# Local attention in units of 32 queries with 128 keys, all 8 heads in one piece

## The chip, the core and the metric

The kernel runs on one core of one Trainium2 chip. The metric is the device time of one launch in microseconds (us), median of three runs. The kernel works on five engines with a queue each: PE (TensorE, matmuls; its weight loads are shown as PEld), DVE (VectorE), ACT (ScalarE), POOL (GpSimd) and SP (SyncE), which here issues nearly all DMA transfers.

## The reference

```python
B, H, Sl, D, Sg = 4, 8, 512, 64, 32; window = 32; scale = 1 / np.sqrt(D)
# global queries see all keys, local queries see the global keys and |i - j| <= 32
s_g = scale * q_g @ concat(k_g, k_l).T;  out_g = softmax(s_g) @ concat(v_g, v_l)
s_ll = np.where(mask, scale * q_l @ k_l.T, -1e9)
s_l = concat(scale * q_l @ k_g.T, s_ll)
out_l = softmax(s_l) @ concat(v_g, v_l)
x = concat(out_g, out_l) as [2176 tokens, 512]
# first feed-forward: d_model 512, d_ff 2048
h = x @ w_in;  y = (h * tanh(softplus(h))) @ w_out
# then 8 experts of 272 tokens each: a greedy assignment by the logits y @ w_gate,
# and relu(y @ w1[e]) @ w2[e] for the tokens of each expert
```

All is float32. The change touches `out_l` alone.

## The kernel before

Phase 1 (the function `phase1`, here 0 to some 310 us) does the attention and the first half of the first feed-forward (8 of 16 rows of 128 hidden units) for six of its blocks; phase 2 (to some 500 us) does the rest of that feed-forward; then come the routing and the experts. Everything behind phase 1 is untouched by the change and runs off what phase 1 leaves.

The 2048 local queries are 16 tiles of 128 (t = 0 to 15). A tile is worked in two **pieces** of 4 heads (`piece(t, g)`). A piece has stages, each ended by a `yield`: (q) scores psS = Q K^T of 128 queries with 224 keys (its own 128, 32 global, 32 on either side), one matmul a head, two heads at a time in the two halves of the array's rows (L357); (t) DVE adds the mask and takes the row's maximum (L367); (e, f) ACT takes exp and the row's sum (L371); (n) DVE divides the probabilities by the sum (L375 to L378); (a, A, b, B) PE transposes them, in 128 and 96 keys, and ACT copies each set of four to SBUF (L382 to L392); (v) the product with v as weights, two matmuls a head, gives the output transposed in psX (L401, L402); (y) ACT and DVE split it into a high and a low float32r part, xh and xl (`x_parts`, L343, L345). Eight pieces for the global queries (`piece_g`) stand between them.

The weights of the feed-forward come as 16 loads of 512 KB in phase 1 (`load_wide`): a DMA into one of three buffers `wide` (L215), three DVE instructions that unpack (L220 to L222), and a split on ACT and POOL (L195, L198). A **chunk** is a quarter of a block's feed-forward: matmuls into psH (L509), a chain on ACT and DVE (L517 to L535) and matmuls into psY (L543). It is given to PE in four **units**; its weights must have been loaded. A **gate** multiplies a finished block's tile by w_gate (L268 to L280).

The order of work is a loop in `phase1` (L649) over the pieces, with a table `SEQ` (`SEQ1` for the first NS = 7 rounds) of what to emit in a round: "4z" is stage z of the piece begun four rounds ago, "u" a unit, "g" a gate's step, "w" idle matmuls that keep PE awake. RATE (L662) says how many units a round may emit, LDR and LDR1 (L659) how many loads. In the first NS rounds PE, ACT and DVE work in the order of emission, after them PE alone does; the other two are ordered by a scheduler. SP keeps its own order, and a DMA that waits holds those behind it.

Of the kernel before, what the change touches and what calls it, by code (L numbers as in the profile page):

```python
# [24 lines left out]
WIN = 32  # L25
TOP = -(1 << 30)
# [15 lines left out]
CH0 = 6  # L42
RATE = 0.667
LDR1 = 1.1
LDR = 1.5
LAG = 1
XTRA = 6
WK = ["001", "301", "113", "211"]
CHAIN = 5
SEQ = "4z u 2A 0n u 2B 3x g U"  # L50
SEQ1 = "0q w 1f 2a 2A w 3v 0t 3y 3x 1n w 2b 0e 2B"
STAGES = "qtefnaAbBvyxz"
NS = 7
# [18 lines left out]
def constants():  # L72
    c = {}
    c["ident"] = np.eye(128)
    c["triu"] = np.triu(np.ones((128, 128)), 1)
    c["off"] = np.tile(np.arange(KT) - (KT - 1) // 2, (128, E))
    c["ecol"] = np.tile(np.arange(E) * 256, (128, 1))
    c["eadj"] = np.tile(REST - 256 - np.arange(E) * (256 - CAP + 256), (128, 1))
    c["iob"] = np.tile(np.r_[0:256, REST:REST + 128], (128, 1))
    c["ioa"] = np.tile(np.arange(NT) * 128, (128, 1))  # L80
    row = token_rows()
    c["rhi"] = row // 128
    c["rlo"] = row % 128
    c["frev"] = (N * E - (row[:, :, None] * E + np.arange(E))).reshape(128, -1)
    i = np.arange(128)[:, None]
    mask = []
    for first, last in ((True, False), (False, False), (False, True)):
        j = np.arange(128)[None]
        r = np.arange(32)[None]
        ok = np.concatenate([abs(i - j) <= WIN, np.ones((128, SG), bool),  # L90
                             (i <= r) & (not first), (r <= i - 96) & (not last)], 1)
        mask.append(np.where(ok, 0.0, NEG))
    c["mask"] = np.concatenate(mask, 1)
# [12 lines left out]
def lay_out(q_l, k_l, v_l, q_g, k_g, v_g):  # L106
    qk = np.zeros((B, 4, 128, 4, 352), np.float32)
    v = np.zeros((B, 4, 128, 2, DM), np.float32)
    qg = np.zeros((B, 2, 128, 2, SG), np.float32)
    kt = np.zeros((B, 2, 128, 2, SL + SG), np.float32)  # L110
    vt = np.zeros((B, 2, 128, 4, 256), np.float32)

    def pairs(a):
        return a.reshape(B, 4, 2, a.shape[2], D).transpose(0, 2, 4, 1, 3).reshape(B, 128, 4, a.shape[2])

    def rows(a):
        return a.transpose(0, 2, 1, 3).reshape(B, a.shape[2], DM)

    ql, kl, kg = pairs(q_l), pairs(k_l), pairs(k_g)
    vl, vg = rows(v_l), rows(v_g)  # L120
    for c in range(4):
        s = c * 128
        qk[:, c, :, :, 0:128] = ql[..., s:s + 128]
        qk[:, c, :, :, 128:256] = kl[..., s:s + 128]
        qk[:, c, :, :, 256:288] = kg
        v[:, c, :, 0] = vl[:, s:s + 128]
        v[:, c, 0:32, 1] = vg
        if c > 0:
            qk[:, c, :, :, 288:320] = kl[..., s - 32:s]
            v[:, c, 32:64, 1] = vl[:, s - 32:s]  # L130
        if c < 3:
            qk[:, c, :, :, 320:352] = kl[..., s + 128:s + 160]
            v[:, c, 64:96, 1] = vl[:, s + 128:s + 160]
    qa = pairs(q_g)
    for g in range(2):
        qg[:, g] = qa[:, :, 2 * g:2 * g + 2]
        kt[:, g, :, :, :SL] = kl[:, :, 2 * g:2 * g + 2]
        kt[:, g, :, :, SL:] = kg[:, :, 2 * g:2 * g + 2]
        vt[:, g] = vl[:, :, g * 256:(g + 1) * 256].reshape(B, 4, 128, 256).transpose(0, 2, 1, 3)
    return {"qk": qk, "v": v, "qg": qg, "kt": kt, "vt": vt}  # L140


class Build:
# [203 lines left out]
    def piece(s, t, g):  # L347
# [14 lines left out]
        mx = s.sp.tile([128, 4], F32, name="mx")
        sm = s.sp.tile([128, 4], F32, name="sm")
        for hp in range(2):
            for j in range(2):
                h = 2 * hp + j
                s.link(nc.vector.tensor_tensor_reduce(out=P[:, h], in0=psS[j][:, hp], in1=mask, scale=-SCALE, scalar=3e38,  # L367
                                                      op0=OP.add, op1=OP.min, accum_out=mx[:, h:h + 1]))
        yield "t"
        for h in range(4):  # L370
            s.link(nc.scalar.activation(P[:, h], P[:, h], AF.Exp, bias=mx[:, h:h + 1], scale=-1.0,  # L371
                                        accum_out=sm[:, h:h + 1]))
            if h > 0:
                yield " eef"[h]
        s.link(nc.vector.tensor_scalar(sm, sm, 1e-9, None, op0=OP.add))  # L375
        s.link(nc.vector.reciprocal(sm, sm))
        for h in range(4):
            s.link(nc.vector.tensor_scalar(P[:, h], P[:, h], sm[:, h:h + 1], None, op0=OP.mult))  # L378
        yield "n"
        psA = s.psT.tile([128, 4, 128], F32, name="psA", tag="t")  # L380
        for h in range(4):
            s.link(nc.tensor.transpose(psA[:, h], P[:, h, 0:128], s.ident))  # L382
        yield "a"
        PA = s.ap.tile([128, 4, 128], F32, name="PA")
        s.link(nc.scalar.activation(PA, psA, AF.Copy))
        yield "A"
        psB = s.psT.tile([96, 4, 128], F32, name="psB", tag="t")
        for h in range(4):
            s.link(nc.tensor.transpose(psB[:, h], P[:, h, 128:224], s.ident))
        yield "b"  # L390
        PB = s.ap.tile([96, 4, 128], F32, name="PB")
        s.link(nc.scalar.activation(PB, psB, AF.Copy))  # L392
        yield "B"
        if g == 0:
            s.px = s.psT.tile([128, 4, 128], F32, name="psX", tag="x")
        px, v = s.px, s.V[t]
        for h in range(4):
            hp, j = 2 * g + h // 2, h % 2
            d0 = (2 * hp + j) * 64
            o = px[j * 64:(j + 1) * 64, hp]  # L400
            s.link(nc.tensor.matmul(o, v[:, 0, d0:d0 + 64], PA[:, h], start=True, stop=False))  # L401
            s.link(nc.tensor.matmul(o, v[:96, 1, d0:d0 + 64], PB[:, h], start=False, stop=True))  # L402
        if g == 0:
            return
# [26 lines left out]
    def load_gv(s, i):  # L431
# [7 lines left out]
        nc.sync.dma_start(vg, vd[b, 0, 0:32, 1, g * 256:(g + 1) * 256])  # L439
        s.gv = v, vg  # L440

    def piece_g(s, i):
# [16 lines left out]
        P = s.ap.tile([128, 544], F32, name="Pg", tag="P", bufs=3)  # L459
# [11 lines left out]
        PA = s.ap.tile([128, 4, 128], F32, name="PgA", tag="PA")  # L471
# [5 lines left out]
        PB = s.ap.tile([32, 128], F32, name="PgB", tag="PB")  # L477
# [108 lines left out]
    def phase1(s, p1):  # L586
# [3 lines left out]
        for t in range(16):  # L590
            pieces += [("l", t, 0), ("l", t, 1)] + [("g", i) for i, a in enumerate(GLOBALS) if a == t]
        chunks = [(bi, f) for bi in range(6) for f in range(0, FP, 2)]
        with ExitStack() as at:
# [18 lines left out]
            s.mask = s.gp.tile([128, 3, 224], F32, name="mask")  # L612
# [33 lines left out]
            n = sent = 0  # L646
            acc = 0.0
            old = []
            while pieces or old:  # L649
# [5 lines left out]
                new = None  # L655
                if pieces:
                    p = pieces.pop(0)
                    new = s.piece(*p[1:]) if p[0] == "l" else s.piece_g(p[1])
                while loads and sent <= (n * LDR1 if n < NS else NS * LDR1 + (n - NS) * LDR):  # L659
                    s.side.append(loads.pop(0))  # L660
                    sent += 1
                acc = min(acc + RATE * 4, 6) if n >= CH0 else 0  # L662
# [3 lines left out]
                w = iter(WK[n] if n < len(WK) else ())  # L666
                for op in (SEQ1 if n < NS else SEQ).split():
                    if op == "w":
                        idle(int(next(w, 0)))
# [6 lines left out]
                    elif op == "g":  # L676
                        if s.gates:
                            g = s.gates[0]
                            s.gate((s.at.get(g, 0),))
                            if s.at[g] == 1:  # L680
                                s.gate((1,))
                    elif int(op[0]) < len(old) and old[int(op[0])]:
# [3 lines left out]
                s.turn_all(s.side)  # L686
                while old and (len(old) > 4 or (old[-1] is None)):
                    old.pop()
                if n == 1:
                    s.load_v(1)  # L690
                    nc.sync.dma_start(s.wg[:, :4 * E].rearrange("p (k e) -> p k e", e=E), s.ins["wg"].rearrange("(k p) e -> p k e", p=128))
                if n == 4:
# [543 lines left out]
```

## Time and profile before

| | us |
|---|---|
| runs: median (lowest to highest of 3) | 862.93 (860.92 to 863.78) |
| the profiled execution: its time / its span | 863.93 / 862.1 |
| PE busy over the span | 801.1 (93%) |
| DVE, ACT, POOL busy | 580.5 (67%), 455.9 (53%), 170.5 (20%) |
| HBM read / written | 91.00 MB / 19.66 MB |

Busy time of matmuls is the union of their modelled spans, so a PE that reads 99% may still have matmuls further apart than they need be; what a group of matmuls costs is read from the start of the first to the start of what follows. An f32 matmul stands in the trace as two instructions (a transpose as one).

### The profile page before, as it was taken

What the parts mean: (1) busy time and instruction counts of PE and PEld (TensorE: products, weight loads), DVE (VectorE), ACT (ScalarE), POOL (GpSimd) and SP (SyncE); (2) the same over time, 40 slices, a digit from 0 to 9 for tenths busy, and PEclk for the clock granted to TensorE, in tenths of its full rate; (3) what the DMA queues carried; (4) which work ended last, traced back from release to release, by engine and by line L of the source; (5) the groups of instructions that cost most, each with busy time, mean ns of one, the idle gap of its engine ahead of it and who ended that gap; (6) DMA issues with size and microseconds to landing.
All of it is one profiled execution on the core that took longest, in us unless ns stands there. A gap on an engine that the chain in (4) does not pass through costs nothing. (4 is left out here: it accounts for less than half of the span.)

```text
span 862.1 us, 16222 instructions
## 1 busy us (share of the span) xinstructions
PE 801.1 (93%) x6276; PEld 688.6 (80%) x6276; DVE 580.5 (67%) x1467; ACT 455.9 (53%) x987; POOL 170.5 (20%) x138
## 2 busy tenths in 40 slices
PE   8787999999999999979999997899879899999995
PEld 4565777777777888868999876677679899999994
DVE  6999866656666458797877868886646565564420
ACT  5676666666676656556555653222246454454320
POOL 1222100000000012243100146644330221222001
PEclk9899999999999999999999999999999999999998
DMA  9768635344441002343131114423557646665101
GB/s 316 252 212 283 201 135 170 100 145 125 161 137 52 25 25 74 99 133 100 50 97 52 51 49 140 62 29 46 159 152 242 218 139 229 208 210 194 50 8 55
DMA packets 44720, 111.74 MB, mean 130 GB/s; under 512 B 5728, under 2 KB 14304, under 8 KB 44640
## 3 DMA queue, kind: packets, MB, share of 16 engines
q1 hardware_dynamic: 37696, 91.01, 32.5%
q0 software_dynamic: 6944, 19.67, 9.0%
q8 instruction: 50, 0.82, 0.4%
q14 instruction: 30, 0.25, 0.1%
HBM read 91.00 MB, written 19.66 MB: 128 GB/s over the span
## 5 line engine op out<-in xcount | busy, mean ns | idle before, releaser
L517 ACT ACTIVATE me<-psH 128x512 f32<-128x512 f32 (+1 forms) x72 | 41.0, 570 | 60.0 <-PE psH L509 59.9
L371 ACT ACTIVATE P<-P,mx 128x224 f32<-128x224 f32 x128 | 60.1, 470 | 19.6 <-DVE mx L367 19.1
L519 DVE TENSOR_SCALAR mu<-me 128x512 f32<-128x512 f32 (+1 forms) x72 | 34.9, 484 | 36.7 <-ACT me L517 35.6
L522 ACT ACTIVATE me<-mu,two 128x512 f32<-128x512 f32 (+1 forms) x72 | 49.9, 693 | 15.5 <-DVE mu L520 15.0
L525 DVE TENSOR_TENSOR mu<-mu,psH 128x512 f32<-128x512 f32 (+1 forms) x72 | 46.9, 652 | 10.9 <-ACT me L522 10.8
L367 DVE CUSTOM_DVE_ANT_0 P<-psS,mask 128x224 f32<-128x224 f32 x128 | 43.1, 385 | 8.8 <-PE psS L357 8.6
L520 DVE SCALAR_TENSOR_TENSOR mu<-me,mu 128x512 f32<-128x512 f32 (+1 forms) x72 | 47.6, 661 | 1.9
L1190 DVE SCALAR_TENSOR_TENSOR hl<-ps2H,hh 128x272 fp32r<-128x272 f32 x64 | 27.0, 437 | 27.9 <-ACT hh L1189 27.9
L1189 ACT ACTIVATE hh<-ps2H 128x272 fp32r<-128x272 f32 x64 | 24.8, 395 | 38.9 <-PE ps2H L1187 38.8
L198 POOL TENSOR_TENSOR wo10l<-wz,wo10h 128x512 fp32r<-128x512 f32 x2 | 2.6, 1323 | 214.0 <-ACT wo10h L195 214.0
L523 ACT ACTIVATE me<-me 128x512 f32<-128x512 f32 (+1 forms) x72 | 43.6, 606 | 1.5
L357 PE MATMUL psS<-qk 64*128 64x224 f32 x256 | 38.9, 384 | 3.6 <-DVE L L583 2.3
L378 DVE TENSOR_SCALAR P<-P,sm 128x224 f32<-128x224 f32 x128 | 36.9, 351 | 1.0
L1204 ACT ACTIVATE oT<-ps2O 128x256 f32<-128x256 f32 x32 | 12.1, 378 | 41.9 <-PE ps2O L1202 41.9
L357 PEld LDWEIGHTS psS<-qk 64*128 64x128 f32 x256 | 24.8, 190 | 11.8 <-issue 4.5
L1168 POOL DMA_INDIRECT out<-ro,idx x17 | 21.4, 1259 | 60.8 <-ACT ro L1167 47.2
L1205 DVE COPY orest<-ps2O 128x16 f32<-128x16 f32 x32 | 5.5, 172 | 39.1 <-ACT oT L1204 36.2
L527 DVE TENSOR_TENSOR g<-mu,me 128x512 f32<-128x512 f32 (+1 forms) x36 | 27.2, 755 | 4.2 <-ACT me L523 0.3
L535 DVE TENSOR_TENSOR gl<-mw,gh 128x512 fp32r<-128x512 f32 (+1 forms) x36 | 26.7, 740 | 4.3 <-ACT gh L533 4.2
L401 PE MATMUL psX<-PA,v 128*64 128x128 f32 x256 | 28.8, 295 | 0.0
L533 ACT ACTIVATE gh<-mw 128x512 fp32r<-128x512 f32 (+1 forms) x36 | 21.7, 603 | 12.8 <-DVE mw L532 12.6
L382 PE MATMUL psA<-ident,P 128*128 128x128 f32 x128 | 21.7, 285 | 6.4 <-DVE P L378 4.2
(933 smaller groups left out, 3011.6 us busy)
## 6 DMA issues: line engine op xcount, KB each, us to landing
stage<-w SPq DMA_DIRECT2D x64, 512.0 KB, 4.2
qk<-qk SPq DMA_DIRECT2D x16, 704.0 KB, 5.3
v<-v SPq DMA_DIRECT2D x16, 512.0 KB, 4.7
wide<-w_in SPq DMA_DIRECT2D x16, 512.0 KB, 5.1
wide<-w_out SPq DMA_DIRECT2D x16, 512.0 KB, 5.3
kgl<-kt SPq DMA_DIRECT2D x8, 544.0 KB, 4.0
vgl<-vt SPq DMA_DIRECT2D x8, 512.0 KB, 4.4
y_d<-y1o SPq DMA_DIRECT2D x16, 256.0 KB, 2.7
```

The source lines that it names most:

```text
L357: s.link(nc.tensor.matmul(psS[j][:, hp], q[:, :128], q[:, 128:], start=True, stop=True))
L367: s.link(nc.vector.tensor_tensor_reduce(out=P[:, h], in0=psS[j][:, hp], in1=mask, scale=-SCALE, scalar=3e38, op0=OP.add, op1=OP.min, accum ...
L371: s.link(nc.scalar.activation(P[:, h], P[:, h], AF.Exp, bias=mx[:, h:h + 1], scale=-1.0, accum_out=sm[:, h:h + 1]))
L378: s.link(nc.vector.tensor_scalar(P[:, h], P[:, h], sm[:, h:h + 1], None, op0=OP.mult))
L401: s.link(nc.tensor.matmul(o, v[:, 0, d0:d0 + 64], PA[:, h], start=True, stop=False))
L517: s.link(nc.scalar.activation(e, ps, AF.Exp))
L519: s.link(nc.vector.tensor_scalar(u, e, E20, 2.0, op0=OP.min, op1=OP.add))
L520: s.link(nc.vector.scalar_tensor_tensor(u, e, E20, u, op0=OP.min, op1=OP.mult))
L522: s.link(nc.scalar.activation(e, u, AF.Ln, bias=s.two))
L523: s.link(nc.scalar.activation(e, e, AF.Exp, scale=-1.0))
L525: s.link(nc.vector.tensor_tensor(u, u, ps, op=OP.mult))
L527: s.link(nc.vector.tensor_tensor(w, u, e, op=OP.mult))
```

## The change

A tile is now one piece of all 8 heads. Its 128 queries are four units of 32. A unit's 128 keys are its own 32, 32 on either side and the 32 global ones: `SPAN` lists the blocks of 32 keys of a tile in an order in which each unit's four stand together, from `FIRST[u]` on. A score matmul has 32 queries of one head as weights and writes 32 partitions of psS (32 matmuls a tile). The exps are not normalised; they are transposed by head (8 transposes), and the product takes 32 columns of the transposed probabilities as weights and v as the moving side (32 matmuls a tile), so that queries lie on the partitions; DVE multiplies this by the reciprocal sums, and four transposes bring it into the layout of before. The arrays `qk` and `v` repeat keys and values for this: 960 KB and 1024 KB a tile. The table of the order, the rates and the depth (a piece ends in the round after its own) are new too; the two loads of a round are emitted at its two "s". Numbers after "L" of the changed kernel are its own lines.

```diff
+SPAN = ("G", -1, 0, 1, 2, "G", 1, 2, 3, 4, "G")
+FIRST = (0, 2, 5, 7)
+QK = 128 + 32 * len(SPAN)
-CH0 = 6
-RATE = 0.667
+CH0 = 3
+RATE = {"l": 5.2, "g": 3.0}
-SEQ = "4z u 2A 0n u 2B 3x g U"
+SEQ0 = "0q w 1A 0t w 1B 1v s 0e w 1x 0f 1z s 0n"
+SEQ = "u 1A 0n u s 1B 1v u s g u 1x g u s 1z g U"
-NS = 7
+NS = 3
...
-    qk = np.zeros((B, 4, 128, 4, 352), np.float32)
-    v = np.zeros((B, 4, 128, 2, DM), np.float32)
+    qk = np.zeros((B, 4, 128, 4, QK), np.float32)
+    v = np.zeros((B, 4, 128, 4, DM), np.float32)
...
-    def piece(s, t, g):
+    def piece(s, t):
...
+        psS = [pool.tile([128, 4, 128], F32, name="psS") for _ in range(2)]
+        for hp in range(4):
+            for u, f in enumerate(FIRST):
+                r = slice(u * 32, u * 32 + 32)
+                for j in range(2):
+                    q = qk[j * 64:(j + 1) * 64, hp]
+                    s.link(nc.tensor.matmul(psS[j][r, hp], q[:, r], q[:, 128 + f * 32:256 + f * 32], start=True, stop=True))
+        s.load_qk(t + 2)
...
+        for h in range(8):
+            s.link(nc.vector.tensor_tensor_reduce(out=P[:, h], in0=psS[h % 2][:, h // 2], in1=mask, scale=-SCALE, scalar=3e38,
+                                                  op0=OP.add, op1=OP.min, accum_out=mx[:, h:h + 1]))
...
-        for h in range(4):
-            s.link(nc.vector.tensor_scalar(P[:, h], P[:, h], sm[:, h:h + 1], None, op0=OP.mult))
...
+        for z, (y, w) in enumerate(("aA", "bB")):
+            ps = s.psT.tile([128, 4, 128], F32, name="psA", tag="t")
+            for h in range(4):
+                s.link(nc.tensor.transpose(ps[:, h], P[:, 4 * z + h], s.ident))
...
+            s.link(nc.scalar.activation(PT[z], ps, AF.Copy))
...
+        psO = s.psT.tile([128, 8, D], F32, name="psO", tag="x")
+        for h in range(8):
+            for u in range(4):
+                r = slice(u * 32, u * 32 + 32)
+                s.link(nc.tensor.matmul(psO[r, h], PT[h // 4][:, h % 4, r], v[:, u, h * D:(h + 1) * D], start=True, stop=True))
+        s.load_v(t + 2)
...
+        s.link(nc.vector.tensor_tensor(O, psO, sm[:, :, None].to_broadcast([128, 8, D]), op=OP.mult))
...
+        for hp in range(4):
+            s.link(nc.tensor.transpose(px[:, hp], O[:, 2 * hp:2 * hp + 2].rearrange("p h d -> p (h d)"), s.ident))
...
-                while loads and sent <= (n * LDR1 if n < NS else NS * LDR1 + (n - NS) * LDR):
-                    s.side.append(loads.pop(0))
+                    elif op == "s":
+                        if loads:
+                            s.side.append(loads.pop(0))
+                        s.turn_all(s.side)
```

On PE, the attention of half a tile in a round of before (P and psS are of different pieces; units stand where the lines are left out):

```order
L382 MATMUL psA<-ident,P 128x128 x4
L357 MATMUL psS<-qk 128x224 x4
...
L389 MATMUL psB<-ident,P 96x128 x4
L401 MATMUL psX<-PA,v 64x128
L402 MATMUL psX<-PB,v 64x128
```

and that of a whole tile in a round of the changed kernel:

```order
L390 MATMUL psA<-ident,P 128x128 x4
L367 MATMUL psS<-qk 32x128 x32
...
L390 MATMUL psA<-ident,P 128x128 x4
L400 MATMUL psO<-v,PAA 32x64 x16
L400 MATMUL psO<-v,PAB 32x64 x16
...
L408 MATMUL psX<-ident,O 128x128 x4
```

The scores are 32 instead of 8 matmuls a tile, and the product is two runs of 16, the second of which reads the copy PAB of the transposes right before the first.

On DVE at the start, before (the first tile's last reduction with its maximum, the division, the first load's unpacking, the next reduction):

```order
L367 ISA P,mx<-psS,mask 128x224
L367 ISA mx 128x1
L375 TENSOR_SCALAR sm<-sm 128x4
L376 RECIPROCAL sm<-sm 128x4
L378 TENSOR_SCALAR P<-P,sm 128x224 x4
L220 TENSOR_SCALAR wz<-wide 128x512
L221 SCALAR_TENSOR_TENSOR wz<-wide,wz 128x512
L222 SCALAR_TENSOR_TENSOR wz<-wide,wz 128x512
L367 ISA P,mx<-psS,mask 128x224
```

and in the changed kernel:

```order
L374 ISA P,mx<-psS,mask 128x128
L374 ISA mx 128x1
L228 TENSOR_SCALAR wz<-wide 128x512
L229 SCALAR_TENSOR_TENSOR wz<-wide,wz 128x512
L230 SCALAR_TENSOR_TENSOR wz<-wide,wz 128x512
L383 TENSOR_SCALAR sm<-sm 128x8
L384 RECIPROCAL sm<-sm 128x8
L374 ISA P,mx<-psS,mask 128x128
L374 ISA mx 128x1
```

The division of P is gone, and the first load's three instructions moved ahead of the sums and of the next tile's reductions.

On SP at the start, before:

```order
L334 DMA qk<-qk 128x1408
L339 DMA v<-v 128x1024
L215 DMA wide<-w_in 128x4x256
L334 DMA qk<-qk 128x1408
L215 DMA wide<-w_in 128x4x256
L339 DMA v<-v 128x1024
L691 DMA wg<-wg 128x4x8
L215 DMA wide<-w_out 128x1024
L334 DMA qk<-qk 128x1408
```

and in the changed kernel:

```order
L342 DMA qk<-qk 128x1920
L347 DMA v<-v 128x2048
L342 DMA qk<-qk 128x1920
L223 DMA wide<-w_in 128x4x256 x2
L347 DMA v<-v 128x2048
L694 DMA wg<-wg 128x4x8
L342 DMA qk<-qk 128x1920
L347 DMA v<-v 128x2048
L223 DMA wide<-w_out 128x1024 x2
```

The third tile's qk moved ahead of the first load, and the first two loads stand together.

## Rows read from the trace of the kernel before

**Rows 1.** stretches of phase 1: us, then busy us of each engine, clock, DMA
```profile
0.00:40.00 40.00, 31.30 (x202) 19.27 (x204) 31.67 (x116) 23.97 (x75) 7.48 (x9) 0.91 0.81 280
40.00:100.00 60.00, 49.49 (x436) 38.47 (x434) 57.27 (x164) 40.34 (x105) 15.72 (x11) 0.97 0.71 237
100.00:200.00 100.00, 98.41 (x855) 78.07 (x855) 65.48 (x225) 67.50 (x182) 0.00 (x0) 1.00 0.47 149
200.00:310.00 110.00, 108.87 (x1036) 87.93 (x1029) 66.58 (x209) 69.94 (x181) 2.61 (x2) 1.00 0.27 87
```

**Rows 2.** PE in order of time, a round: start us, us, instructions merged
```profile
140.60 0.60 PE L389 MATMUL psB<-ident,P 128*96 128x128 f32 x4
141.13 0.45 PE L401 MATMUL psX<-PA,v 128*64 128x128 f32 x4
...
142.21 0.43 PE L276 MATMUL psl<-rT,wg 128*32 128x128 f32 x8
...
153.30 1.03 PE L357 MATMUL psS<-qk 64*128 64x224 f32 x8
154.26 0.39 PE L509 MATMUL psH<-x2h,wi01h 128*128 128x256 f32 x1
```

**Rows 3.** matmuls with 32-column weights, PE in order of time
```profile
58.77 1.06 PE L451 MATMUL psS<-kgl,qg 64*32 64x512 f32 x8
59.65 0.24 PE L451 MATMUL psG<-kgl,qg 64*32 64x32 f32 x8
```

**Rows 4.** weight loads of 32 columns, PE's loads in order of time
```profile
82.72 0.84 PEld L486 LDWEIGHTS psO<-vgl,PgA 128*32 128x32 f32 x32 [0.36 <-DVE sm L375]
```

**Rows 5.** one line's instructions: ns min/median/max
```profile
L451 PE MATMUL psS<-kgl,qg x64: 589/613/1047, 58.8 to 267.2; 64*32 64x512 f32 x64
...
L451 PE MATMUL psG<-kgl,qg x64: 189/192/258, 59.7 to 267.6; 64*32 64x32 f32 x64
```

**Rows 6.** DVE in order of time at the start
```profile
7.01 0.39 DVE L367 CUSTOM_DVE_ANT_0 P<-psS,mask 128x224 f32<-128x224 f32 x1
...
7.32 0.39 DVE L367 CUSTOM_DVE_ANT_0 P<-psS,mask 128x224 f32<-128x224 f32 x1
...
9.22 0.17 DVE L375 TENSOR_SCALAR sm<-sm 128x4 f32<-128x4 f32 x1
...
9.64 1.07 DVE L378 TENSOR_SCALAR P<-P,sm 128x224 f32<-128x224 f32 x4
...
24.92 0.69 DVE L345 TENSOR_TENSOR x0l<-psX,x0h 128x512 fp32r<-128x512 f32 x1
```

**Rows 7.** DVE groups of 0 to 100 us: busy us, mean ns of one
```profile
L221 DVE SCALAR_TENSOR_TENSOR wz<-wide,wz 128x512 int32<-128x512 int32 x18 | 15.4, 854 | 0.2
L222 DVE SCALAR_TENSOR_TENSOR wz<-wide,wz 128x512 int32<-128x512 int32 x18 | 13.7, 764 | 0.3
L220 DVE TENSOR_SCALAR wz<-wide 128x512 int32<-128x512 int32 x18 | 7.9, 444 | 1.3 <-DMA wide<-w_in 1.3
```

**Rows 8.** DVE in order of time at the sixteenth load's end
```profile
89.24 0.67 DVE L222 SCALAR_TENSOR_TENSOR wz<-wide,wz 128x512 int32<-128x512 int32 x1
...
90.20 0.39 DVE L367 CUSTOM_DVE_ANT_0 P<-psS,mask 128x224 f32<-128x224 f32 x1
```

**Rows 9.** ACT groups of phase 1: busy us, mean ns of one, idle before
```profile
L371 ACT ACTIVATE P<-P,mx 128x224 f32<-128x224 f32 x128 | 60.1, 470 | 19.6 <-DVE mx L367 19.1
...
L392 ACT ACTIVATE PB<-psB 96x512 f32<-96x512 f32 x32 | 18.6, 581 | 3.9 <-PE psB L389 3.9
```

**Rows 10.** the DMA engines early, stretches of 2 us
```profile
4.00:6.00 2.00, 2.00 (x9) 0.67 (x8) 0.00 (x0) 0.00 (x0) 0.00 (x0) 1.00 1.05 375
```

**Rows 11.** DMA issues: transfers, KB each, us to landing
```profile
qk<-qk SPq DMA_DIRECT2D x16, 704.0 KB, 5.3
v<-v SPq DMA_DIRECT2D x16, 512.0 KB, 4.7
```

**Rows 12.** SP in order of time: the sixteenth load's issue
```profile
79.50 0.33 SPq L215 DMA_DIRECT2D wide<-w_out  x1
```

More of the change, by code (lines that the diff above doesn't have):

```diff
@@ L84, in constants @@
     c["frev"] = (N * E - (row[:, :, None] * E + np.arange(E))).reshape(128, -1)
[L85 to L93, printed above, removed]
+    mask = np.zeros((128, 3, 4, 32))
+    i = np.arange(32)[:, None]
+    r = np.arange(32)[None]
+    for u, o in enumerate(FIRST):
+        for n, b in enumerate(SPAN[o:o + 4]):
+            if b != "G":
+                for k, gone in enumerate((-1, None, 4)):
+                    ok = (abs(u * 32 + i - b * 32 - r) <= WIN) & (b != gone)
+                    mask[u * 32:u * 32 + 32, k, n] = np.where(ok, 0.0, NEG)
+    c["mask"] = mask.reshape(128, -1)
     lay, o = {}, 0
@@ L121, in lay_out @@
     for c in range(4):
[L122 to L133, printed above, removed]
+        qk[:, c, :, :, 0:128] = ql[..., c * 128:c * 128 + 128]
+        for n, x in enumerate(SPAN):
+            o = 128 + n * 32
+            if x == "G":
+                qk[:, c, :, :, o:o + 32] = kg
+            elif 0 <= 4 * c + x < 16:
+                qk[:, c, :, :, o:o + 32] = kl[..., (4 * c + x) * 32:(4 * c + x + 1) * 32]
+        for u, f in enumerate(FIRST):
+            for n, x in enumerate(SPAN[f:f + 4]):
+                if x == "G":
+                    v[:, c, n * 32:n * 32 + 32, u] = vg
+                elif 0 <= 4 * c + x < 16:
+                    v[:, c, n * 32:n * 32 + 32, u] = vl[:, (4 * c + x) * 32:(4 * c + x + 1) * 32]
     qa = pairs(q_g)
@@ L362, in piece @@
[L362 to L368, printed above, removed]
+        pool = s.psE[t % len(s.psE)]
+        psS = [pool.tile([128, 4, 128], F32, name="psS") for _ in range(2)]
@@ new lines, in piece @@
+        for hp in range(4):
+            for u, f in enumerate(FIRST):
+                r = slice(u * 32, u * 32 + 32)
[3 more added lines that the diff above has]
+        s.load_qk(t + 2)
+        yield "q"
+        P = s.ap.tile([128, 8, 128], F32, name="P", bufs=2)
+        mx = s.sp.tile([128, 8], F32, name="mx")
+        sm = s.sp.tile([128, 8], F32, name="sm")
@@ L375, in piece @@
+        yield "f"
         s.link(nc.vector.tensor_scalar(sm, sm, 1e-9, None, op0=OP.add))
         s.link(nc.vector.reciprocal(sm, sm))
-        for h in range(4):
-            s.link(nc.vector.tensor_scalar(P[:, h], P[:, h], sm[:, h:h + 1], None, op0=OP.mult))
         yield "n"
[L380 to L404, printed above, removed]
+        PT = []
+        for z, (y, w) in enumerate(("aA", "bB")):
+            ps = s.psT.tile([128, 4, 128], F32, name="psA", tag="t")
+            for h in range(4):
+                s.link(nc.tensor.transpose(ps[:, h], P[:, 4 * z + h], s.ident))
+            yield y
+            PT.append(s.ap.tile([128, 4, 128], F32, name="PA" + "AB"[z], tag="P" + "AB"[z], bufs=1))
+            s.link(nc.scalar.activation(PT[z], ps, AF.Copy))
+            yield w
@@ L405, in piece @@
+        psO = s.psT.tile([128, 8, D], F32, name="psO", tag="x")
+        v = s.V[t]
+        for h in range(8):
+            for u in range(4):
+                r = slice(u * 32, u * 32 + 32)
+                s.link(nc.tensor.matmul(psO[r, h], PT[h // 4][:, h % 4, r], v[:, u, h * D:(h + 1) * D], start=True, stop=True))
         s.load_v(t + 2)
         yield "v"
+        O = s.ap.tile([128, 8, D], F32, name="O", bufs=1)
+        s.link(nc.vector.tensor_tensor(O, psO, sm[:, :, None].to_broadcast([128, 8, D]), op=OP.mult))
@@ L458, in piece_g @@
         yield "t"
-        P = s.ap.tile([128, 544], F32, name="Pg", tag="P", bufs=3)
+        P = s.ap.tile([128, 544], F32, name="Pg", tag="P", bufs=2)
         sm = s.sp.tile([128, 4], F32, name="smg")
@@ L590, in phase1 @@
         for t in range(16):
-            pieces += [("l", t, 0), ("l", t, 1)] + [("g", i) for i, a in enumerate(GLOBALS) if a == t]
+            pieces += [("l", t)] + [("g", i) for i, a in enumerate(GLOBALS) if a == t]
         chunks = [(bi, f) for bi in range(6) for f in range(0, FP, 2)]
@@ L611, in phase1 @@
             s.load_qk(0)
-            s.mask = s.gp.tile([128, 3, 224], F32, name="mask")
+            s.mask = s.gp.tile([128, 3, 128], F32, name="mask")
             nc.sync.dma_start(s.mask, s.ins["cst"][:, 128:].rearrange("p (m k) -> p m k", m=3))
@@ L644, in unit @@
                 return True
[L646 removed]
+            n = 0
             acc = 0.0
@@ L654, in phase1 @@
                     s.psY = [p1.enter_context(tc.tile_pool(name="psY", bufs=2, space=PSUM, side="right"))] * 2
[L655 to L658, printed above, removed]
-                while loads and sent <= (n * LDR1 if n < NS else NS * LDR1 + (n - NS) * LDR):
-                    s.side.append(loads.pop(0))
-                    sent += 1
-                acc = min(acc + RATE * 4, 6) if n >= CH0 else 0
+                p = pieces.pop(0) if pieces else ("g", None)
+                new = None if p[1] is None else s.piece(p[1]) if p[0] == "l" else s.piece_g(p[1])
+                acc = min(acc + RATE[p[0]], 8) if n >= CH0 else 0
                 old[:0] = [new]
@@ L676, in phase1 @@
                     elif op == "g":
[L677 to L680, printed above, removed]
+                        cur = s.gates[0] if s.gates and cur == 0 else cur
+                        k = s.at.get(cur, 0)
+                        if cur in s.gates:
+                            s.gate((k,))
+                            if k == 0:
                                 s.gate((1,))
+                        cur = cur or None
                     elif int(op[0]) < len(old) and old[int(op[0])]:
@@ L685, in phase1 @@
                             at_stage[g] = STAGES.index(next(g, "z"))
[L686 to L689, printed above, removed]
+                del old[1:]
+                if new is None:
+                    old = []
+                if n == 0:
                     s.load_v(1)
                     nc.sync.dma_start(s.wg[:, :4 * E].rearrange("p (k e) -> p k e", e=E), s.ins["wg"].rearrange("(k p) e -> p k e", p=128))
-                if n == 4:
+                if n == 3:
                     s.load_gk(0)
```

40 lines of the change are left out of this document (15 added, 25 removed).

## The prediction

> **What bounds the kernel now.** I read the stretches of phase 1 first: the reader is to see two regimes. From 0 to 100 us PE is busy 81 of 100 us while DVE, from 40 us on, is busy 57.3 of 60; from 100 to 310 us PE is busy 207 of 210 and DVE 132 [rows 1]. So the first 100 us go at DVE's pace, and what follows at PE's. Then PE's order of time, for what a round's attention costs there; DVE's order of time and groups at the start; ACT's groups; and last the DMA engines and SP, since the change moves more data. Behind phase 1 nothing is touched, so I take the time from the end of phase 1 to the end as it is and ask by how much phase 1 ends earlier.
>
> **PE, part by part.** Four transposes take from 140.60 to 141.13, 0.53 us; the product of half a tile from 141.13 to 142.21, 1.08 us; the scores of half a tile from 153.30 to 154.26, 0.96 us [rows 2]. A tile costs 2 x (0.53 + 1.08 + 0.53 + 0.96) = 6.2 us of PE.
>
> The changed kernel needs three sets of four transposes (two of P, one of O): 1.6 us. The product has 32 matmuls, 64 instructions, with weights of 32 columns and 64 moving columns. The global pieces of before do the same kind: 32 such weight loads in 0.84 us, 26 ns each [rows 4]. 64 x 0.026 = 1.7, with 0.1 for the first to come through 1.8 us; against the two old products, 2.2 us, a gain, but a small one.
>
> The scores have 32 matmuls, 64 instructions, of 128 moving columns, in two halves of the rows times four groups of 32 columns. No row has eight such tiles beside each other. The nearest: eight instructions of 512 columns in four column groups, rows alternating, take 1.06 us with 0.61 for one, and what follows starts 0.88 us after the first (59.65 - 58.77) [rows 3, 5]; that is four abreast, 0.44 us a wave. Eight instructions of 128 columns take 0.43 us [rows 2]. From below: eight abreast, a wave of 128 columns at a quarter of 0.44, 0.11 us; 64 / 8 = 8 waves, 0.9 us, with the start 1.0. From above, if instructions come no closer than the 26 ns of rows 4: 1.7 us. Far above, if column groups gave nothing beside the row halves: the old scores are 8 instructions of 224 columns in 0.96 us, 0.069 us for 128 columns, 64 x 0.069 = 4.4 us. I take 1.3, between the first two, since rows 3 show column groups at work with alternating rows.
>
> The Trainium skill has a rule against this, in "TensorE: Matmul & The Clock Gate", section "Wait — 56ns, not 53.3ns?": start-to-start of matmuls never drops below some 25 ns, however few columns they have. The trace disagrees for column groups: eight matmuls of 32 columns are over in 0.24 us though one takes 0.19 [rows 3, 5], so seven starts share some 50 ns. By the rule the scores would be 64 x 0.025 = 1.6 us, an estimate, and the sum less by some 3 us in the ten tiles below; this is near the second case.
>
> A tile is then 1.6 + 1.8 + 1.3 = 4.7 us, 1.5 less. Ten tiles (t = 6 to 15) lie in PE's regime: 15 us. The change adds one wait: the second half of the product reads the copy PAB of the transposes that stand right ahead of it, and everything behind it on PE waits with it. The copy takes 0.58 us [rows 9], the first half of the product covers 0.9; what is left is ACT's queue, where an exp of 0.47 us or a like instruction may be in front. ACT is busy two thirds [rows 1]. I take 0.3 us a tile (bounds 0 and 1.0), 3 us. The multiplication by the sums lies behind two units, some 3 us, ahead of the transposes of O, and costs PE nothing while DVE is busy two thirds; without that cover it would be its 0.7 us a tile. **PE's regime: 15 - 3 = 12 us earlier.**
>
> **DVE and the start.** A reduction with its maximum comes every 0.31 us; four divisions take 1.07 us; the sums of a piece 0.42 (9.22 to 9.64); xl 0.69 [rows 6]. A tile is 8 x 0.31 + 2 x 1.07 + 2 x 0.42 + 0.69 = 6.15 us. After: eight reductions of 128 instead of 224 columns, between 0.31 x 128 / 224 = 0.18 and 0.31, I take 0.21: 1.7; one set of sums, 0.42; the multiplication from PSUM, 512 columns as xl, 0.69; xl 0.69: 3.5 us. Saved 2.65 us a tile. The loads stay at 0.85 + 0.76 + 0.44 = 2.1 us each [rows 7]. The sixteenth is done at 89.9 us, with six tiles reduced (the seventh starts at 90.2) [rows 8]: 6 x 2.65 = 16 us saved by then.
>
> Against it stands DVE's new order: the first load's unpacking comes right behind the first reductions, and its DMA now has the third qk ahead of it. Ahead of and with it go three qk of 960 KB, mask and identity of 256, v of 1024, the load's 512: 4672 KB, 4.8 MB. The engines reach 375 GB/s [rows 10]; from a start near 2 us (an estimate: the issue and the slow first us) that is 2 + 4.8 / 0.375 = 14.8 us. DVE is done with the first reductions near 6.9 + 1.7 = 8.6 (the first scores stand behind the ten warm-up matmuls as before), so it waits 6 us, and the reductions of tile 1 behind it; at the third load some 2.5 us more by the same count. **The start: 16 - 8.5, some 8 us earlier.**
>
> **DMA.** Per tile qk grows from 704 to 960 KB and v from 512 to 1024 [rows 11], 12.6 MB in all. Up to the sixteenth load SP's order has 8 qk, 7 v, 16 loads, four stores of x, two global sets: 22.1 MB before, 27.7 after. Before, the sixteenth is issued at 79.5 [rows 12], so 22 MB took some 83 us, 266 GB/s. At 375 the 27.7 MB need 74 us: enough, if SP keeps the engines fed. I cost it at nothing beyond the waits above, hidden behind DVE's 70 us of work there; without that cover it is the second rival.
>
> **Sum.** The profiled execution took 863.9 us (span 862.1), 1.0 above the median of the runs. 863.9 - 12 - 8 = 844; in terms of the median, 843.
>
> **Rivals.**
> - *Small matmuls come at 26 ns, and the copy is always waited for.* Scores 1.8 us and the full 1.0 us at PAB: a tile then saves 0 us net in PE's regime, and the start alone stays: 863.9 - 8 = 856, less if one of the two holds, 850 to 857. For it: rows 4. Against: rows 3.
> - *The start goes at the DMA engines' pace, slower than before.* SP's queue is in order, and a transfer that waits for a buffer holds all behind it; the rate was 266 GB/s with that. At this rate 27.7 MB take 104 us, the sixteenth load comes 20 us later than before, and PE's 12 us later on don't pay for it: 863.9 + 20 - 12 = 872. It decides below 27.7 / (83 + 12) = 290 GB/s. For it: the engines' share of 0.7 to 0.8 in the first 100 us at 237 to 280 GB/s [rows 1]. Against: at that time DVE was what the loads' buffers waited for, and it is quicker now.
> - *The column groups don't run beside each other in the scores:* 4.4 us, a tile 7.8 instead of 6.2, 16 x 1.6 = 26 us later, 890. Against: rows 3.
> - *DVE's saving comes through in full,* the waits for the first loads being made up for before PE needs them, with the scores at 1.0 us and no wait at PAB: 16 at the start, 10 x 1.8 later: 830, or 826 with some gain in the early tiles on PE.
>
> **How the numbers follow.** Forecast 0.60, its own range 833 to 853; the first rival 0.14; DMA 0.13 (858 to 875, from no change to slower); no column groups 0.03; the full saving 0.10. The range of 8 in 10 reaches from 826 to 860. Faster by over 0.3% (2.6 us, about what a measurement of this kernel can tell from no change): 0.60 + 0.14 + 0.10 = 0.84; within 0.3%: 0.05 of the DMA case; slower: its other 0.08 and 0.03, 0.11.
>
> **What would show it.** Right: scores near 1.0 to 1.7 us and product near 1.8 us from start to start on PE; DVE idle some 6 us ahead of the first L228, released by the DMA of `wide`; the sixteenth load unpacked near 82 us; the last xl of phase 1 some 20 us earlier than before, and the same time from there to the end. Wrong: PE idle behind PAB by about 1 us a tile; the DMA share near 1 until the sixteenth load and that later than 90 us; or phase 2 longer than before, which I hold to be untouched.

## The result and the profile after

The changed kernel takes 873.45 us (median of 5 runs, 868.8 to 875.33), the kernel before 863.78 us beside it (860.92 to 866.21): a ratio of 1.0101, 95% interval 1.0062 to 1.014. It is 1% slower. The forecast was 843 us, with 826 to 860 as the range. The profiled execution of the changed kernel is the fastest of its five, 868.8 us with a span of 867.0, 4.9 above the span before; its trace understates the loss by some 5 us.

The stretches of phase 1 in the changed kernel (us, then the busy time of PE, PEld, DVE, ACT, POOL with the instruction counts, the granted clock, the DMA share and GB/s):

```profile
0.00:40.00 40.00, 24.17 (x392) 14.76 (x393) 17.43 (x76) 16.41 (x59) 5.28 (x8) 0.83 0.91 336
40.00:100.00 60.00, 44.93 (x624) 37.86 (x623) 46.72 (x124) 33.72 (x93) 15.24 (x12) 0.80 0.76 268
100.00:200.00 100.00, 85.34 (x1175) 70.04 (x1175) 51.24 (x168) 54.06 (x157) 0.67 (x1) 0.91 0.50 173
200.00:310.00 110.00, 102.92 (x1476) 82.66 (x1475) 63.00 (x200) 68.69 (x196) 0.00 (x0) 0.98 0.41 142
```

The reader is to compare the last two with [rows 1]. From 100 to 310 us PE was busy 207 of 210 us; now it is busy 188, and its clock is 0.91 and 0.98 where it was 1.00. DVE is no longer full from 40 to 100 us, as forecast, but PE and DVE now both stand idle there for about a quarter of the time.

What PE waits for from 100 to 310 us, first before, then after (who waits for whom: us in total, times, longest):

```profile
PE psS L357 <- DVE L L583: 2.3, 8, 0.3
PE psY L543 <- DVE gl L535: 0.5, 1, 0.5
PE psX L493 <- DVE Og L490: 0.4, 1, 0.4
```

```profile
PE psO L400 <- ACT PAB L393: 10.5, 5, 3.9
PE psO L488 <- ACT PgB L480: 7.5, 7, 1.5
PE psrT L276 <- DVE mx L374: 2.5, 1, 2.5
```

Three microseconds of waiting have become 21, and 18 of them are for two copies of transposed probabilities: PAB of the local tiles and PgB of the global pieces. One such wait, on PE and then on ACT, in order of time:

```profile
140.10 0.60 PE L390 MATMUL psA<-ident,P 128*128 128x128 f32 x4
140.63 1.16 PE L367 MATMUL psS<-qk 64*32 64x128 f32 x64
141.72 0.51 PE L545 MATMUL psY<-wo03h,gh 128*128 128x512 f32 x1
...
143.22 0.60 PE L390 MATMUL psA<-ident,P 128*128 128x128 f32 x4
143.75 0.65 PE L400 MATMUL psO<-v,PAA 128*32 128x64 f32 x32
148.32 0.65 PE L400 MATMUL psO<-v,PAB 128*32 128x64 f32 x32 [3.92 <-ACT PAB L393]
148.91 0.50 PE L545 MATMUL psY<-wo03h,gh 128*128 128x512 f32 x1
```

```profile
143.87 0.40 ACT L378 ACTIVATE P<-P,mx 128x128 f32<-128x128 f32 x1 [0.30 <-DVE mx L374]
...
144.47 0.63 ACT L535 ACTIVATE gh<-mw 128x512 fp32r<-128x512 f32 x1
145.00 0.39 ACT L378 ACTIVATE P<-P,mx 128x128 f32<-128x128 f32 x1
...
147.31 0.39 ACT L378 ACTIVATE P<-P,mx 128x128 f32<-128x128 f32 x1
...
147.70 0.57 ACT L393 ACTIVATE PAB<-psA 128x512 f32<-128x512 f32 x1
```

The second transposes of P are done by 143.82. Their copy could run then. It stands on ACT behind all eight exps of the next tile, which the round emits ahead of it ("0n" before "1B" in `SEQ`), and those can't begin before DVE's reductions of scores that PE made at 140.63. So the copy runs at 147.70, and PE, in order, stands still for 3.92 us.

### The profile page after: what moved, and what is told of

Read it like the earlier page. It is cut to its first block, busy times and chain, and to the rows that moved or that the text cites. A ratio compares the mean times of both kernels' runs of the same rounds, so it can differ in the third digit from the quotient of the medians.

```text
span 867.0 us, 18491 instructions
## 1 busy us (share of the span) xinstructions
PE 777.0 (90%) x7496; PEld 675.3 (78%) x7496; DVE 537.8 (62%) x1323; ACT 429.5 (50%) x955; POOL 168.6 (19%) x138
## 5 line engine op out<-in xcount | busy, mean ns | idle before, releaser
L378 ACT ACTIVATE P<-P,mx 128x128 f32<-128x128 f32 x128 | 49.5, 388 | 12.8 <-DVE mx L374 12.8
L527 DVE TENSOR_TENSOR mu<-mu,psH 128x512 f32<-128x512 f32 (+1 forms) x72 | 47.0, 653 | 12.3 <-ACT me L524 11.6
L374 DVE CUSTOM_DVE_ANT_0 P<-psS,mask 128x128 f32<-128x128 f32 x128 | 28.7, 284 | 13.8 <-PE psS L367 13.7
L535 ACT ACTIVATE gh<-mw 128x512 fp32r<-128x512 f32 (+1 forms) x36 | 21.7, 603 | 11.6 <-DVE mw L534 11.2
L408 PE MATMUL psX<-ident,O 128*128 128x128 f32 x64 | 11.9, 317 | 16.7 <-DVE O L404 16.7
L400 PE MATMUL psO<-v,PAB 128*32 128x64 f32 x512 | 11.3, 233 | 17.1 <-ACT PAB L393 16.6
L534 DVE TENSOR_TENSOR mw<-mu,me 128x512 f32<-128x512 f32 (+1 forms) x36 | 25.0, 693 | 2.1 <-ACT me L525 0.8
L228 DVE TENSOR_SCALAR wz<-wide 128x512 int32<-128x512 int32 x32 | 16.7, 522 | 14.4 <-DMA wide<-w_in 10.3
L229 DVE SCALAR_TENSOR_TENSOR wz<-wide,wz 128x512 int32<-128x512 int32 x32 | 24.8, 774 | 0.3
```

Of the source, the lines that this page charges most:

```text
L374: s.link(nc.vector.tensor_tensor_reduce(out=P[:, h], in0=psS[h % 2][:, h // 2], in1=mask, scale=-SCALE, scalar=3e38, op0=OP.add, op1=OP.mi ...
L527: s.link(nc.vector.tensor_tensor(u, u, ps, op=OP.mult))
```

## The experiments

**The exps behind the copy.** One edit to the changed kernel: the reductions and the exps of the new tile are emitted behind the copy PAB. TensorE's order within a round stays.

```
-SEQ = "u 1A 0n u s 1B 1v u s g u 1x g u s 1z g U"
+SEQ = "u 1A 0q u s 1B 0n 1v u s g u 1x g u s 1z g U"
```

> Order of emission alone: the reductions and exps of the new tile are emitted behind the copy PAB of the old one (from the fourth round on); the order on PE in a round stays. Copy theory (PE's regime is lost to the wait for PAB and PgB, which stand behind eight exps on ACT; 24 us of waits on PE between 0 and 310 us of the changed kernel): most of these waits go, 10 to 15 us faster than the changed kernel, 858 to 863. Start theory (the loss is in the first 100 us: the first load stands ahead of the sums on DVE, and PE sleeps and is granted the lower clock): no change, 870 to 875. Bytes theory (12.6 MB more slow the start): no change, 870 to 875.

Measured: 844.52 us (843.39 to 845.31), ratio to before 0.9775, 0.975 to 0.9801. That is 29 us under the changed kernel, more than the theory asked for. Its waits from 100 to 310 us and its stretch from 140 to 200 us, with that of the changed kernel behind it:

```profile
PE psO L400 <- ACT PAB L393: 4.3, 7, 1.6
PE psO L488 <- ACT PgB L480: 1.2, 1, 1.2
```

```profile
140.00:200.00 60.00, 56.33 (x837) 46.31 (x838) 33.66 (x117) 39.34 (x120) 0.00 (x0) 1.00 0.60 216
```

```profile
140.00:200.00 60.00, 49.26 (x665) 40.71 (x664) 25.75 (x92) 30.07 (x89) 0.00 (x0) 0.86 0.42 149
```

The two waits fall by 12.5 us, and the clock is back at 1.00. Both come back with one edit, so this run alone does not part them; nor does it part the exps on ACT from the reductions on DVE, which moved with them.

**Loads later at the start.** No load's unpacking ahead of the first sums and of O on DVE.

```
-SEQ0 = "0q w 1A 0t w 1B 1v s 0e w 1x 0f 1z s 0n"
+SEQ0 = ["0q w 1A 0t w 1B 1v 0e w 1x 0f 1z s 0n" + k * " s" for k in range(3)]
...
-for op in (SEQ0 if n < NS else SEQ).split():
+for op in (SEQ0[n] if n < NS else SEQ).split():
```

> The first three rounds emit 1, 2 and 3 load steps at their end instead of 2 each in their middle, so that no unpacking stands ahead of a tile's sums, reductions or the product's multiplication. Copy theory: 1 to 3 us faster than the changed kernel at most, 869 to 873. Start theory: PE's wait of 8.5 us for O near 23 us and the low clock behind it go, 6 to 10 us faster, 863 to 868. Bytes theory: no change, since the sixteenth load comes no earlier.

Measured: 875.66 us (873.44 to 882.41), ratio 1.0143, 1.0106 to 1.018. PE's wait for O in phase 1 falls from 16.7 to 8.0 us and nothing is gained: the start theory, in this form, has fallen.

**Both edits together.**

> Both edits. Copy theory: as the first alone, 857 to 862. Start theory: as the second alone, 863 to 868. If both hold, the gains add: 850 to 856. Bytes theory: 870 to 875.

Measured: 847.37 us (840.89 to 851.92, without one run of 3444.33), ratio 0.9801, 0.9756 to 0.9845: no better than the first edit alone, as the run before says.

**Half a dose.** Four exps ahead of the copy, four behind.

```
-SEQ = "u 1A 0n u s 1B 1v u s g u 1x g u s 1z g U"
+SEQ = "u 1A 0e u s 1B 0n 1v u s g u 1x g u s 1z g U"
```

> Half a dose of the first experiment: four of the eight exps of the new tile ahead of the copy PAB on ScalarE, four behind it; TensorE's order as in the changed kernel. Theory (the copy stands in ScalarE's queue behind the exps): four exps at 0.39 us are 1.6 us of the wait of up to 3.9 us a tile, so the time lies between the changed kernel (873.5) and the one with all eight behind (844.5): 850 to 864 us, PE's waits for PAB between 8 and 14 us. Rival (what counts is that VectorE does the new tile's reductions before the old tile's end, or another effect of the round's order, not the exps): these stand as in the changed kernel, 870 to 877 us.

Measured: 848.0 us (846.54 to 848.6), ratio 0.9811, 0.9786 to 0.9837; the rival's 870 to 877 is out. The reductions stand ahead of the copy here too, so it is the exps that count. The waits for PAB and PgB from 100 to 310 us are 6.1 and 2.4 us; those for PAB alone are 10.5 over all of phase 1, in the forecast band. The time is below it: half the exps gave back 25 of the 29 us. The loss is not proportional to the number of exps in front, and neither are the waits: 18.0, 8.5 and 5.5 us with eight, four and none emitted in front.

**Filling the wait.** The wait is left, the first half of the product is done three times.

```
-        for h in range(8):
+        for h in [0, 1, 2, 3] * (3 if t > 5 else 1) + [4, 5, 6, 7]:
```

> The changed kernel, the wait for PAB left as it is, but TensorE does the first half of the product three times over in tiles 6 to 15 (the same values again, 2 x 0.74 us of more work a tile), so that it stands idle less. Theory A (a good part of the loss is TensorE's clock, which the trace shows lowered to 0.83 to 0.91 of full speed from 140 to 200 us, after the idle stretches): the clock stays at 1.00 there, some 10 us come back, less up to 4 us of the added work where the wait is under 1.5 us: 862 to 870 us. Theory B (the loss is the idle time itself, and the clock costs little): the clock may rise but the time doesn't fall: 872 to 880 us.

Measured: 873.23 us (868.12 to 875.46), ratio 1.0114, 1.0087 to 1.0142: the time of the changed kernel, so theory A's 862 to 870 is missed. But the stretch shows what A says of the clock:

```profile
140.00:200.00 60.00, 51.17 (x921) 42.75 (x912) 29.06 (x100) 33.45 (x98) 0.00 (x0) 0.97 0.52 180
```

0.97 instead of 0.86, with PE busier. The added work is less than the 2 x 0.74 us a tile that I had expected:

```profile
199.00 1.55 PE L400 MATMUL psO<-v,PAA 128*32 128x64 f32 x96
200.36 0.63 PE L400 MATMUL psO<-v,PAB 128*32 128x64 f32 x32
```

Three first halves take 1.36 us to the next start where a single one takes 0.58, so ten tiles have some 8 us more, and these cost no time. About 4 of them stood in the wait for PAB (10.5 to 6.6 us). For the rest an estimate of what the clock gives back, made as the one below for the changed kernel, is of the right size: 51.2 x 0.03 + 101.8 x 0.02 = 3.6 us lost to it here (0.98 from 200 to 310 us, as in the changed kernel) against 9, so 5 back. Theory A had sized the gain too high; that the clock follows the idle stretches is shown, what it costs is still an estimate.

**The copy on the other engine.** TensorE's order and the exps ahead of the transposes as in the changed kernel; DVE makes the copy PAB of tiles 6 to 15. The sums of the new tile, which on DVE would wait for the exps ahead of the copy, are emitted behind it.

```
-SEQ = "u 1A 0n u s 1B 1v u s g u 1x g u s 1z g U"
+SEQ = "u 1A 0f u s 1B 0n 1v u s g u 1x g u s 1z g U"
...
-            s.link(nc.scalar.activation(PT[z], ps, AF.Copy))
+            s.link(nc.vector.tensor_copy(PT[z], ps) if z and t > 5 else nc.scalar.activation(PT[z], ps, AF.Copy))
```

> The changed kernel with its order on TensorE, and the eight exps still ahead of the second transposes, but the copy PAB of tiles 6 to 15 made by VectorE, where it stands behind the eight reductions (0.21 us each) and not behind the exps (0.39 us each, which begin only after the reductions). Theory (it is the queue of the engine that copies, not the order on TensorE, that the product waits for): the waits for PAB from 100 to 310 us fall from 10.5 to under 6 us, those for PgB stay at 7.5, and the time is 853 to 862 us. Rival (any copy in this place is late, or the order is to blame in another way): 868 to 877 us.

Measured: 862.22 us (859.06 to 866.05), ratio 0.9994, 0.9974 to 1.0015, at the edge of the theory's band and out of the rival's.

```profile
PE psO L488 <- ACT PgB L480: 7.3, 7, 1.5
PE psO L400 <- DVE PAB L393: 5.8, 6, 2.9
```

The copy itself is slower on DVE (0.69 us) than on ACT (0.60, the medians), and yet 11 us come back: it is the queue in front of it. PgB, still on ACT behind the exps, waits as before.

**Fewer bytes.** The first experiment with 704 KB of qk and 512 KB of v a tile; the key groups and halves of v are read double, so the attention isn't the reference's.

```
-            s.Q[t] = s.ap.tile([128, 4, QK], F32, name="qk")
+            s.Q[t] = s.ap.tile([128, 4, 352], F32, name="qk")
-            s.V[t] = s.ap.tile([128, 4, DM], F32, name="v")
+            s.V[t] = s.ap.tile([128, 2, DM], F32, name="v")
```

> The first experiment (exps behind PAB) with the tile loads cut to the bytes of the kernel before: of qk 704 KB and of v 512 KB are loaded, the key groups and halves of v are read double, so the attention is not that of the reference, at the same instructions. Theory A (the first 100 us go at the DMA engines' pace, 27.7 MB where 22.1 went before): the sixteenth load comes 5 to 15 us earlier than the first experiment's, 830 to 840 us. Theory B (the start's pace is set by the chain between the engines and by the clock, not by bytes): 842 to 847 us.

Its 1116.57 us can't be used: the work behind 500 us depends on the values, and with these it takes far longer (from 600 to 850 us PE is busy 43 us, at a granted clock of 0.50). Phase 1 can be read. The sixteenth load's last instruction on DVE, the seventh tile's first reduction and the last xl, the first experiment's rows ahead of this one's:

```profile
97.18 0.69 DVE L230 SCALAR_TENSOR_TENSOR wz<-wide,wz 128x512 int32<-128x512 int32 x1
...
114.59 0.29 DVE L374 CUSTOM_DVE_ANT_0 P<-psS,mask 128x128 f32<-128x128 f32 x1 [1.43 <-PE psS L367]
...
289.85 0.69 DVE L353 TENSOR_TENSOR x7l<-psX,x7h 128x512 fp32r<-128x512 f32 x1 [0.77 <-ACT x7h L351]
```

```profile
83.71 0.67 DVE L230 SCALAR_TENSOR_TENSOR wz<-wide,wz 128x512 int32<-128x512 int32 x1
...
109.27 0.29 DVE L374 CUSTOM_DVE_ANT_0 P<-psS,mask 128x128 f32<-128x128 f32 x1 [1.56 <-PE psS L367]
...
284.31 0.69 DVE L353 TENSOR_TENSOR x7l<-psX,x7h 128x512 fp32r<-128x512 f32 x1 [0.76 <-ACT x7h L351]
```

The sixteenth load is done at 84.4 instead of 97.9 us, 13.5 earlier, near the upper end of theory A's 5 to 15. The seventh tile comes 5.3 us earlier, and the end of attention 5.5: of the gain at the load that much arrives, and it is what the bytes cost in time. For the kernel before with transfers of the changed kernel's size, which would have shown the bytes alone, there is no time: its SBUF has no room for the larger buffers.

**Idle matmuls at the start,** on top of the first experiment.

```
-SEQ0 = "0q w 1A 0t w 1B 1v s 0e w 1x 0f 1z s 0n"
+SEQ0 = "0q w 1A 0t w 1B 1v s 0e w W 1x 0f 1z s 0n"
...
+                    elif op == "W":
+                        idle((0, 36, 10)[n])
```

> The first experiment with 36 and 10 more idle matmuls in the second and third round, ahead of the transposes that wait 8.8 and 3 us for O, so that TensorE is not idle there. Theory A (the clock of 0.67 to 0.88 from 20 to 100 us costs time): clock near 1.00 from 20 to 60 us and a time of 833 to 840 us. Theory B (VectorE and the loads set the pace of the start, whatever TensorE's clock): 842 to 847 us.

Measured: 843.25 us (841.94 to 844.19), ratio 0.9759, 0.9733 to 0.9785, against 0.975 to 0.9801. The last xl stands at 287.22 instead of 289.85, 2.6 us earlier, but the times are apart by 1.3 us with overlapping intervals: theory B within what these runs can tell. From 0 to 40 us the clock rose from 0.80 to 0.93, from 40 to 100 only from 0.79 to 0.82, so theory A was not fully put to the test.

**A unit between the transposes and the product,** on top of that:

```
+SEQ = "u 1A 0q u s 1B u 0n 1v s g 1x u g u s 1z g U"
```

> The experiment with idle matmuls at the start, and a unit of the expert layer put on TensorE between the second transposes of P and the product that reads their copy PAB (the unit is taken from behind the product, so a round has as many). Theory (what is left of the waits for PAB from 100 to 310 us, 4.4 us, is the copy itself of 0.58 us and what stands in front of it on ScalarE; a unit of some 1.5 us covers it): PAB under 1 us from 100 to 310, 837 to 841 us. Rival (the wait moves to the next copy, PAA or O, whose cover the unit was): 842 to 847 us.

Measured: 842.45 us (840.33 to 847.17), ratio 0.9765, 0.9735 to 0.9795. The rival holds:

```profile
PE psX L408 <- DVE O L404: 7.5, 8, 1.7
...
PE psO L400 <- ACT PAB L393: 0.2, 1, 0.2
```

**The sums behind O,** with that:

```
+SEQ = "u 1A 0q u s 1B u 0f 1v s g 1x u 0n g u s 1z g U"
```

> The experiment with a unit ahead of the product that reads PAB, with the sums of the new tile (which wait for its eight exps) put behind the old tile's O on VectorE. Theory (the wait for PAB moved to O, 7.5 us from 100 to 310, since O stands on VectorE behind work that waits for the new tile's exps): the waits for O fall under 3 us and the time to 835 to 840 us. Rival (O waits for the product itself and for the unit's work on VectorE, not for the sums): waits for O of 5 us or more, 841 to 846 us.

Measured: 840.96 us (836.71 to 845.96), ratio 0.9754, 0.9715 to 0.9794. The wait for O is 7.5 us as without the edit, so the sums weren't what O waited for. The median is the lowest of all, but its interval overlaps that of the first experiment, which stays the smallest edit that beats both kernels.

**The first load's DMA early.** Its issue moved ahead of the second qk, with 12 instead of 36 idle matmuls.

```
+            s.side.append(loads.pop(0))
+            s.turn_all(s.side)
             s.load_qk(1)
             s.load_v(0)
```

> The experiment with idle matmuls at the start (12 instead of 36 in the second round), and the DMA of the first expert load issued behind the first qk instead of behind the third, so that each load is a round earlier. Theory A (VectorE's wait of 8.5 us for that load holds up the start): that wait falls under 2 us, and the time to 833 to 840 us. Theory B (the DMA engines, at a share of 0.9 for the first 40 us, set the pace; what comes earlier for the load comes later for qk and v): 841 to 846 us.

Measured: 844.34 us (841.28 to 846.64), ratio 0.9777, 0.9747 to 0.9806: theory B. DVE's wait for the first load did fall, to 0.6 us, but the second load is now waited for 6.7 us (the first was 8.0 with the idle matmuls alone), and PE's waits for qk rise from 2.3 to 4.0 us. What came earlier for one transfer came later for others. The sixteenth load is done at 91.6 us instead of 95.4, and the last xl is later all the same, 289.92 instead of 287.22.

## Why the prediction was wrong

**The step that failed** is the wait at PAB, "0.3 us a tile (bounds 0 and 1.0), 3 us". I saw the wait, and wrote that "an exp of 0.47 us or a like instruction may be in front". In the order of the changed kernel eight exps are in front whenever the round's new piece is a local tile, and they in turn wait for DVE's reductions. The wait came to 10.5 us over the ten tiles, 1.0 a tile, where the prediction had its upper bound and one of its signs of being wrong; in single tiles it was between nothing and 3.9 us. And the sum named one new wait where there are two: the global pieces' PgB meets the same eight exps, for another 7.5 us. Both together cost PE 18.0 us from 100 to 310 us, against 3 in the sum. Taking the exps from the front gave 29 us back, taking half of them 25, moving the copy to an engine without them 11: the cause is shown three ways.

**What the wait drew after it** was in no step: the clock. An estimate: PE's busy time times what is missing of full clock, 49.3 x 0.14 from 140 to 200 us and 102.9 x 0.02 from 200 to 310, is 9 us. Rows of the same work ahead of the wait of 3.92 us and behind it show how it costs time:

```profile
142.53 0.39 PE L545 MATMUL psY<-wo03h,gh 128*128 128x512 f32 x1
142.76 0.39 PE L545 MATMUL psY<-wo03l,gh 128*128 128x512 f32 x1
...
149.97 0.63 PE L545 MATMUL psY<-wo03h,gh 128*128 128x512 f32 x1
150.40 0.63 PE L545 MATMUL psY<-wo03l,gh 128*128 128x512 f32 x1
```

Ahead of it such a matmul takes 0.23 us to the next start, behind it 0.43, until 152.7 us. That the clock fell there with the idle stretches and was 1.00 without them is shown; the 9 us are an estimate, which the run that filled the wait agrees with but doesn't measure.

**PE's own work** came out better than forecast. Scores take 1.09 us to the next start (140.63 to 141.72) against 1.3, three sets of transposes 1.6 as forecast. A product that is not held up, on PE in order of time:

```profile
13.21 0.65 PE L400 MATMUL psO<-v,PAA 128*32 128x64 f32 x32
13.97 0.65 PE L400 MATMUL psO<-v,PAB 128*32 128x64 f32 x32
14.55 0.61 PE L610 MATMUL psH<-warm 128*128 128x512 bf16 x2
```

0.76 and 0.58 us from start to start, 1.34 against 1.8. A tile is 4.0 us, not 4.7, and ten tiles save 22 us, not 15. The scores' 1.09 us lies near the 1.0 that the prediction worked out for eight tiles abreast, so column groups do run beside each other, and the third rival is out. The first is half right: the copy is waited for by 1.0 us a tile on average, as it says, though not in every tile, but the matmuls don't come at 26 ns; 64 instructions in 1.09 us are 17 ns each. The rule of the Trainium skill weighed in the prediction ("TensorE: Matmul & The Clock Gate", section "Wait — 56ns, not 53.3ns?", some 25 ns from start to start) fails here for column groups, as it did in [rows 3, 5].

From 100 us on this adds up to the loss by itself: -22 of work, +18 of waits (21.4 against 3.2 in all), +9 of clock, about +5, and the span is 4.9 longer. The terms are good for some 2 us and no more: at 100 us the changed kernel has five tiles through the product, the kernel before five and a half.

**The start** gave nothing where 8 us were forecast. DVE did save its work (busy 64 us of the first 100 instead of 89), but the start no longer went at DVE's pace. The sixteenth load's last instruction on DVE ends at 98.6 us (89.9 before, [rows 8]); forecast was 82.

```profile
97.95 0.68 DVE L230 SCALAR_TENSOR_TENSOR wz<-wide,wz 128x512 int32<-128x512 int32 x1
```

At 100 us both kernels have nevertheless done the same expert work, before and after:

```profile
0.00:100.00 100.00, 16.65 (x120) 14.70 (x120) 0.95 0.75 254
```

```profile
0.00:100.00 100.00, 22.91 (x120) 20.55 (x120) 0.81 0.82 295
```

(one line of matmuls alone, L509 and L511: PE and PEld busy, clock, DMA share, GB/s). The wait at the first load was forecast, at 6 us; it is 8.5, and PE's next work waits for O behind it:

```profile
17.36 0.43 DVE L228 TENSOR_SCALAR wz<-wide 128x512 int32<-128x512 int32 x1 [8.52 <-DMA wide<-w_in]
```

```profile
23.65 1.11 PE L408 MATMUL psX<-ident,O 128*128 128x128 f32 x4 [8.49 <-DVE O L404]
```

After that idle stretch four transposes take 1.11 us instead of the 0.60 at 140.10: about the ratio of the two clock levels, 1.2 and 2.4 GHz. Costing 5.6 MB more "at nothing" was the step that failed here: with the bytes of before (the run with fewer bytes, built on the first experiment) the sixteenth load is done at 84.4 us, near the forecast 82, and attention ends 5.5 us earlier. PE's idleness costs up to 2.6 more. That is about the 8, but the two were not run together, and what sets the pace from 40 to 100 us, where neither PE, DVE nor the DMA engines are full, stays open. The second rival, the DMA pace as the reason for "slower", is right that the load comes later than before, by 8.7 us where it said 20, but it has fallen as the reason: the first experiment has the same bytes and nearly the same start (sixteenth load at 97.9 us) and is 2.3% faster than before.

Against the sum, the profiled execution is 25 us too long (4.9 longer than before where 20 shorter was forecast): 15 from the two copies, an estimated 9 from the clock and 8 from the start, less the 7 that PE's work saved beyond the forecast. That the first experiment's 844.5 us is so near the forecast is partly luck: PE's work saved 7 us more than I said, and the start 8 less.

**Behind phase 1** nothing changed, as forecast: from 310 to 500 us PE is busy 183.9 us in both. But the sign that was to show it, the same time from the last xl to the end, misleads: the last xl is 11.6 us later than before (316.76 against 305.19) and the end only 4.9, because the changed kernel has done more expert work by then (577 matmuls into psH and 276 into psY against 557 and 264, some 5 us at full clock). The first load unpacked behind 310 us comes 6.2 us later (331.03 against 324.87).

## What to carry to other kernels

Where a matmul newly reads a copy made just before it, list what stands ahead of that copy on the copying engine in the built order, and what that work in turn waits for; the bound on the wait is that whole queue, not one typical instruction. Emit the copy that the in-order engine waits for ahead of work for the next tile. And a wait on TensorE is to be costed with what it does to the granted clock of the work behind it.

## What the runs showed of the hardware

Matmuls with weights of 64 rows and 32 columns, eight tiles side by side, come at 17 ns an instruction (64 in 1.09 us, 128 moving columns each); with weights of 128 rows and 32 columns and 64 moving columns, at 14 ns (96 in 1.36 us, in the run that filled the wait). The granted clock was 0.86 from 140 to 200 us in the changed kernel, where PE stood idle for up to 3.9 us at a time, and 1.00 in the first experiment, where the same wait was at most 1.6 us. Behind the wait of 3.92 us matmuls of 512 columns were 0.43 us apart instead of 0.23, about the ratio of the two levels, 1.2 and 2.4 GHz. Some 8 us of extra matmuls in the changed kernel raised the clock there to 0.97 and left the time where it was.
